# A fused attention and gated-MLP kernel: high and low parts for three output blocks of the first span, earlier key exponentials and later value loads for the third batch

## The chip, the cores and the metric

The kernel runs on one core of one Trainium2 chip. The metric is the device time of one execution in microseconds. A core has TensorE (PE, with its weight loads as PEld), VectorE (DVE), ScalarE (ACT), GpSimd (POOL) and SyncE (SP); SP and POOL issue the DMA transfers here.

## The reference

Linear attention over 8 batches and 8 heads (576 rows, 64 columns a head) feeds a gated MLP:

```python
q_s = exp(q - max(q, -1)) / (sum over the row + 1e-9)
k_s = exp(k - max(k, rows)) / (sum over the rows + 1e-9)
kv  = einsum('bhsd,bhse->bhde', k_s, v)
x   = einsum('bhsd,bhde->bhse', q_s, kv)       # then (4608, 512)
out = (sigmoid(x @ w_gate) * (x @ w_val)) @ w_out
```

The three weights are drawn as 64-bit floats (512 x 1536, 512 x 1536, 1536 x 512); everything else is float32, and so is the output of 4608 x 512.

## The kernel before, in words

The 4608 tokens are cut into nine spans of 512 (`w` = 0 to 8), the 1536 hidden columns into twelve blocks of 128 (`j`). Each engine works through its instructions in the order in which the program writes them; that order is written out by hand, and waits between engines follow from which tile is read and written where.

**The first span** (line 1024 on) runs the MLP block by block in full float32, because the weights only arrive and are narrowed from 64 to 32 bits while it runs. For one block: `g1_0` (line 672) computes gate and value sums of the block, eight products of 128x512; `g_sig_0` (680, ACT) takes the sigmoid of the gate, `g_mul_0` (684, DVE) multiplies it with the value sums into the tile `h_0`, one block later; `g2_0` (699) multiplies that by the block's rows of `w_out` and adds it into the four PSUM tiles `acc`. PE runs `g1_0` of block j and then `g2_0` of block j-1. The trace records a full float32 product as two instructions.

Beside that, block by block, the weights are made ready:
- `w_low`, `w_top`, `w_join` (146; 153 and 168; 175) narrow gate and value weights on DVE, ACT and DVE; `wo_low`, `wo_top`, `wo_join` do it for `w_out`.
- `wo_hi` (224, ACT) copies a `w_out` block to a high part, `wo_lo` (228, DVE) subtracts it for a low part, and `wo_store` (234, POOL) writes both to memory for the later spans. `wo_save` is the last two.
- after blocks 2, 5, 7, 9, 10 and 11, `split_hi` (284, ACT) and `split_lo` (289, DVE) split gate and value weights and their sums into high and low parts. The sums' parts sit in `s_sb`, and POOL stores them (294).

**The later spans** multiply such parts in three products (high x high, high x low, low x high) in a faster mode of PE: `g1` (line 717) does gate and value of two blocks at a time by seven sub-products B11, T1, T2, B21, T3, B22, T4 instead of eight, on weights `a_w` and sums `s_sb`; `g2` (785) does the output. A span takes six such stages. POOL reloads `s_sb` for the next stage (301) when a sub-product has read it, and `wo_hl`, `wo_t` (248) for the output.

**The attention of the next span** is woven between: for the second span, at the end of a block, `after_first` (889) puts in `k_mm` (424), the transposition `qf_tr` (549) and `x_mm` (587); at the next block's start `beside_first` (881) puts in `x_ev` (595, ACT copies x out of PSUM) and `qT_split` (562 on ACT, 563 on DVE: high and low part of the scaled q). `g1_0` and the transposition share three PSUM tiles `gv`, so a `g1_0` can start its second half only when the q of its block has been split. For the third batch `load_next` loads the transposed keys (320, SP), takes their maxima (330, DVE) and exponentials (337, ACT) two heads' pairs at a time, and at its step 5 loads q, k and the values v (481, 355, 368, all SP). The values are read by `k_mm` in the third stage of the second span.

SP takes its loads and stores in program order, too: an issue that waits holds all that stand behind it.

Of the kernel before, what the change touches and what calls it, by code (L numbers as in the profile page):

```python
# [8 lines left out]
F32 = mybir.dt.float32  # L9
F32R = mybir.dt.float32r  # L10
# [4 lines left out]
ALU = mybir.AluOpType  # L15
AX = mybir.AxisListType

P = 128
# [3 lines left out]
T = 512  # L22
# [4 lines left out]
NJ = DF // P  # L27
# [24 lines left out]
def attn_moe(ctx: ExitStack, tc: tile.TileContext, qf, qn, qT, k, kT, v, wg, wv, wo, out):  # L52
    nc = tc.nc
# [9 lines left out]
    two = ctx.enter_context(tc.tile_pool(name="two", bufs=2))  # L63
# [20 lines left out]
    v_two = [const.tile([P, DM], F32, name=f"v_{i}") for i in range(2)]  # L84
# [8 lines left out]
        out=kv_sb.rearrange("p b i h e -> p (b i) (h e)"),  # L93
        in_=kv_0.rearrange("p h e -> p (h e)").unsqueeze(1).broadcast_to([P, 4, DM]),
# [22 lines left out]
    wo_t = {}  # L117
# [32 lines left out]
    def narrow_sign(raw):  # L150

        half = raw.bitcast(F16).rearrange("p (e f) -> p e f", f=4)
        nc.scalar.activation(
            half[:, :, 1], words(raw)[:, :, 1].bitcast(F32), AF.Copy, scale=2.0 ** -100
        )
# [8 lines left out]
    def narrow_abs(raw, w):  # L164
        src = words(raw)[:, :, 1].bitcast(F32)
        if len(w.shape) == 3:
            src = src.rearrange("p (a b) -> p a b", a=w.shape[1])
        nc.scalar.activation(w, src, AF.Abs, scale=2.0 ** -112)
# [24 lines left out]
    def w_top(j):  # L193
        narrow_sign(w_raw[j].rearrange("p n e -> p (n e)"))
        for n in range(2):
            narrow_abs(w_raw[j][:, n], w_f32(j, n))

    def w_join(j, *ns):
        for n in ns or range(2):
            narrow_join(w_raw[j][:, n], w_f32(j, n))  # L200
# [9 lines left out]
    def wo_top(j):  # L210
        if j % 2 == 0:
            wo_t[j // 2] = wtpool.tile([P, 2, DM], F32, name="wo_t")
        if not wo_on_vector(j):
            narrow_sign(wo_raw[j])
        narrow_abs(wo_raw[j], wo_t[j // 2][:, j % 2])

    def wo_join(j):
        narrow_join(wo_raw.pop(j), wo_t[j // 2][:, j % 2])

    wo_out = {}  # L220
# [15 lines left out]
    def wo_save(j):  # L236
        wo_lo(j)
        wo_store(j)
# [119 lines left out]
    def v_load(b, t, vt=None):  # L358
        s0, n = KTILES[t]
        if vt is None:  # L360

            if t < 2:
                vt = v_two[t]
            else:
                vt = f_last[:, t - 2].rearrange("p n e -> p (n e)")
        v_sb[b, t] = vt
        src = v[b, s0:s0 + n]
        nc.sync.dma_start(out=vt[:n], in_=src)
# [190 lines left out]
    def qT_split(w, hp):  # L559
        t = qT_sb.pop((w, hp))  # L560
        hi, lo = (ring.tile([P, T], F32R, name="ring") for _ in range(2))
        nc.scalar.copy(out=hi, in_=t)
        nc.vector.tensor_tensor(out=lo, in0=t, in1=hi.bitcast(F32), op=ALU.subtract)
        qT_hl[w, hp] = (hi, lo)
# [95 lines left out]
    acc = {}  # L660


    h_0 = {}
    gate = {}

    def g1_0(j):
        ps = [ps_gv.tile([P, T], F32, name="gv") for _ in range(2)]
# [8 lines left out]
        gate[j] = ps  # L676

    def g_sig_0(j):
        h_0[j] = two.tile([P, T], F32, name="h_0", tag="h_lo")
        nc.scalar.activation(h_0[j], gate[j][0], AF.Sigmoid)  # L680

    def g_mul_0(j):
        g = h_0[j]
        nc.vector.tensor_tensor(out=g, in0=gate.pop(j)[1], in1=g, op=ALU.mult)

    def acc_new(w):
        acc[w] = [ps_acc.tile([P, DM], F32, name="acc") for _ in range(NT)]
# [7 lines left out]
    def g2_0(j):  # L695
        if j == 0:
            acc_new(0)
        for m in range(NT):
            nc.tensor.matmul(  # L699
                acc[0][m], lhsT=h_0[j][:, m * P:(m + 1) * P], rhs=wo_t[j // 2][:, j % 2],  # L700
                start=(j == 0), stop=(j == NJ - 1),
            )
        if j == NJ - 1:
            acc_out(0)

# [146 lines left out]
    def load_next(n, p, vs=range(5)):  # L852

        if n + 1 >= NW:
            return
        b = n + 1 if n + 1 < B else None
        if b is not None:
            if p == 1:
                kT_load(b, 0); kT_load(b, 1)
            if p == 2:  # L860
                k_max(b, 0); k_max(b, 1)
            if p == 3:
                k_sum(b, 0); k_sum(b, 1)
                kT_load(b, 2); kT_load(b, 3)
            if p == 4:
                k_max(b, 2); k_max(b, 3)
                k_max_send(b)
                if n > 1:
                    k_max_read(b)
        if p == 5:  # L870
            for c in range(NC):
                qn_load(n + 1, c)
            if b is not None:
                for t in range(5):
                    k_load(b, t)
                for t in vs:
                    v_load(b, t)

    def beside_first(j):
        if 7 <= j <= 10:
            x_ev(1, j - 7)
        if 6 <= j <= 9:
            qT_split(1, j - 6)
        if j == 6:
            k_done(1)

    def after_first(j):
        if j == 0:  # L890
            for hp in range(NP):
                k_max(1, hp)
            k_max_send(1)
        if j == 1:
            for t in range(5):
                v_load(1, t, v1[t])
            for c in range(NC):
                qn_max(1, c)
            k_max_read(1)
        if j == 2:  # L900
            for c in range(NC):
                qn_sub(1, c)
        if j == 3:
            for c in range(NC):
                qn_exp(1, c)
            for hp in range(NP):
                k_sum(1, hp)
            for t in range(5):
                k_sub(1, t)
        if j == 4:  # L910
            for t in range(5):
                k_exp(1, t)
            for c in range(NC):
                qn_sum(1, c)
        if 4 <= j <= 7:
            qf_mul(1, j - 4)
        if j == 5:
            for t in range(5):
                k_mm(1, t)
        if 6 <= j <= 9:  # L920
            x_mm(1, j - 6)
        if 5 <= j <= 8:
            qf_tr(1, j - 5, ps_gv.tile([P, T], F32, name="gv"))
        if j in (2, 6, 7, 9):
            load_next(1, {2: 1, 6: 2, 7: 3, 9: 4}[j])


    def lend(i):
# [95 lines left out]
    for j in range(NJ - 2):  # L1024
        g1_0(j)
        beside_first(j)
        split = splits.get(j)
        if split is not None:
            split_hi(split)
        if j == 0:  # L1030
            g_sig_0(j)
        else:
            wo_hi(j - 1)
            g_mul_0(j - 1)
        w_top(j + 2)
        if j > 0:
            g_sig_0(j)
        w_join(j + 1)
        wo_top(j + 1)
        wo_join(j)  # L1040
        if j + 3 < NJ:
            w_low(j + 3)
        wo_low(j + 2)
        if j > 0:
            wo_save(j - 1)
        if j + 3 < NJ:
            load_wo(j + 3)
        if j + 5 < NJ - 1:
            load_w(j + 5)
        if j == 7:  # L1050
            load_w(NJ - 1)
        if split is not None:
            split_lo(split)
        if j + 1 in splits:
            w_sums(splits[j + 1])
        if j > 0:
            g2_0(j - 1)
        if j == 3:
            kv_split(0, lambda sl: kv_0[sl, :, sl])
        after_first(j)  # L1060

    j = NJ - 2
# [22 lines left out]
    g_sig_0(j + 1)  # L1085
    split_hi(5, SUMS)
    c_subs()
    load_next(1, 5, range(2))
    c_split_lo(B11)
    split_lo(5, (FIRST,))  # L1090
    split_lo(5, SUMS[0:1])
# [13 lines left out]
    wo_hi(j + 1)  # L1105
    wo_lo(j + 1)
    g2_0(j)
    for t in range(2, 5):
        v_load(2, t)

    def wo_next(w, at):
        wo_load(w, step(w, at))
# [2 lines left out]
    for w in range(1, NW):  # L1115
        last = w == NW - 1
        for at in range(NS):
            p = step(w, at)
            end = last and at == NS - 1
            g1(w, p, None if end else step(w + (at + 1) // NS, (at + 1) % NS))  # L1120
            if prev is None:
                wo_store(NJ - 1)
            ahead = 3 if at == NS - 1 and not last else 0
            for i in range(ahead):
                c_split(i)
            h_split(w, p)
            if ahead:
                for i in range(ahead, 7):
                    c_split(i)
            if not last:  # L1130
                side_a(w + 1, at)
            if prev is None:
                g2_0(NJ - 1)
                wo_hl[1, NS - 1] = [wo_out[j] for j in (NJ - 2, NJ - 1)]
            else:
                g2(*prev)
                if prev == (1, 0):
                    wo_next(1, 1)
                if not end:
                    wo_next(w + (at + 1) // NS, (at + 1) % NS)  # L1140
            prev = (w, at)
            if not last:
                side_b(w + 1, at)
# [39 lines left out]
```

## Time and profile before

| | |
|---|---|
| median of 3 runs | 928.67 us (928.15 to 929.54) |
| the profiled execution's own time | 928.82 us |
| its span, first to last instruction | 927.1 us |
| granted clock of PE | 0.998 |
| PE busy | 919.4 us (99%) |
| DVE, ACT, POOL busy | 619.1, 488.7, 177.2 us |
| moved by DMA | 256.77 MB, 277 GB/s in the mean |

All times in the views count from the first instruction. The first span ends on PE at about 166 us, with the products of line 699 for its last block at 169.5. A busy PE is not PE at its peak: matmuls overlap, and their ends are modelled; the chain of waits gives the time from one group's start to the next.

### The profile page before, as it was taken

The page shows a single profiled execution, that of the slowest core. Times are in us where ns is not written, and L with a number is a line of the kernel's source. Part 1 is how long each engine was busy: PE and PEld are TensorE (multiplying, and loading weights), DVE is VectorE, ACT ScalarE, POOL GpSimd, SP SyncE. Part 2 cuts the span into 40 slices and gives each one's busy share as a digit, 9 for nine tenths or more (in the row PEclk, how much of TensorE's full clock was granted, in tenths as well). Part 3 has the DMA queues.
Part 4 walks back from the last instruction along what each step waited for, and adds up shares of the span by engine and source line. Part 5 has one row for each costly group of instructions (what it writes and reads, how often), then busy time and mean ns, then how long its engine had stood idle before and what let it go on. Part 6 is the DMA issues. An engine that isn't in the chain of part 4 may idle for free.

```text
span 927.1 us, 16312 instructions
## 1 busy us (share of the span) xinstructions
PE 919.4 (99%) x6366; PEld 793.9 (86%) x6366; DVE 619.1 (67%) x1005; ACT 488.7 (53%) x830; POOL 177.2 (19%) x329
## 2 busy tenths in 40 slices
PE   8999999999999999999999999999999999999998
PEld 7445445899999999999999999999999999899997
DVE  7899889865768476757775677656855574654232
ACT  5999885735454544644564456444634443543222
POOL 0011113222121212121221222112211222122220
PEclk9999999999999999999999999999999999999999
DMA  9996676999799969996999699969997799768661
GB/s 331 380 376 255 238 269 238 360 340 283 205 373 323 273 192 372 334 281 183 360 342 282 200 333 333 300 203 310 334 298 219 222 260 317 227 190 257 209 206 68
DMA packets 92507, 256.77 MB, mean 277 GB/s; under 512 B 13648, under 2 KB 13648, under 8 KB 92432
## 3 DMA queue, kind: packets, MB, share of 16 engines
q0 software_dynamic: 46016, 167.27, 57.8%
q1 hardware_dynamic: 46416, 88.48, 31.5%
q8 instruction: 50, 0.82, 0.4%
q14 instruction: 25, 0.20, 0.1%
HBM read 227.15 MB, written 28.56 MB: 276 GB/s over the span
## 4 chain that ended last, share of the span: by engine, by line
PE 98%; DMA 1%; SPq 0%; ACT 0%; issue 0%
PE gv L717 49%; PE acc L785 29%; PE gv L672 9%; PE acc L699 4%; PE at L424 2%; PE gv L587 2%; PE at L587 1%; DMA lent<-v_in 1%; DMA lent<-qf_in 1%; PE gv L549 0%; PE acc L611 0%; PE acc L410 0%; PE at L410 0%; SPq L948 0%; SPq L951 0%; ACT x L691 0%
## 5 line engine op out<-in xcount | busy, mean ns | idle before, releaser
L717 PE MATMUL gv<-c_hl,s_sb 128*128 128x256 f32 x2304 | 277.5, 276 | 0.0
L717 PEld LDWEIGHTS gv<-c_hl,s_sb 128*128 128x128 f32 x2304 | 269.0, 188 | 0.0
L717 PE MATMUL gv<-c_hl,a_w 128*128 128x256 f32 x1728 | 220.9, 277 | 0.0
L717 PEld LDWEIGHTS gv<-c_hl,a_w 128*128 128x128 f32 x1728 | 210.4, 188 | 4.6 <-issue 0.7
L301 POOL DMA_DIRECT2D s_sb<-s x188 | 101.7, 541 | 305.6 <-PE gv L717 297.9
L785 PE MATMUL acc<-wo_hl,h 128*128 128x512 f32 x588 | 142.6, 391 | 0.0
L743 DVE TENSOR_TENSOR sg<-gv,sg 128x512 f32<-128x512 f32 x48 | 33.2, 691 | 158.8 <-PE gv L717 158.8
L785 PE MATMUL acc<-wo_t,h 128*128 128x512 f32 x564 | 138.9, 394 | 0.0
L785 PEld LDWEIGHTS acc<-wo_t,h 128*128 128x128 f32 x564 | 105.8, 188 | 24.8
L785 PEld LDWEIGHTS acc<-wo_hl,h 128*128 128x128 f32 x588 | 106.9, 188 | 20.5
L735 ACT COPY sg<-gv 128x512 f32<-128x512 f32 x48 | 28.1, 586 | 111.0 <-PE gv L717 97.7
L745 ACT COPY sg<-gv 128x512 f32<-128x512 f32 x48 | 28.2, 588 | 102.7 <-PE gv L717 102.7
L747 DVE TENSOR_TENSOR sg<-sg 128x512 f32<-128x512 f32 x48 | 33.3, 693 | 57.3 <-ACT sg L745 57.3
L672 PE MATMUL gv<-x,f_w 128*128 128x512 f32 x160 | 70.4, 593 | 0.0
L248 POOL DMA_DIRECT2D wo_hl<-wo x47 | 27.7, 590 | 182.6 <-PE acc L785 182.6
L672 PEld LDWEIGHTS gv<-x,f_w 128*128 128x128 f32 x160 | 30.0, 190 | 36.6 <-issue 34.4
L768 DVE TENSOR_TENSOR h<-sg,h 128x1024 fp32r<-128x1024 f32 x48 | 58.9, 1226 | 1.6
L756 DVE TENSOR_TENSOR sg<-sg 128x512 f32<-128x512 f32 x48 | 33.3, 693 | 33.6 <-ACT sg L750 33.6
L750 ACT ACTIVATE sg<-sg 128x512 f32<-128x512 f32 x48 | 30.4, 633 | 46.1 <-DVE sg L749 46.1
L740 ACT COPY sg<-gv 128x512 f32<-128x512 f32 x48 | 28.2, 588 | 37.3 <-PE gv L717 37.3
L737 ACT COPY sg<-gv 128x512 f32<-128x512 f32 x48 | 28.2, 588 | 36.3 <-PE gv L717 36.3
L248 POOL DMA_DIRECT2D wo_t<-wo x47 | 25.4, 540 | 99.1 <-PE acc L785 99.0
(148 smaller groups left out, 1120.8 us busy)
## 6 DMA issues: line engine op xcount, KB each, us to landing
s_sb<-s POOLq DMA_DIRECT2D x188, 512.0 KB, 6.4
wo_hl<-wo POOLq DMA_DIRECT2D x47, 512.0 KB, 4.3
wo_t<-wo POOLq DMA_DIRECT2D x47, 512.0 KB, 6.1
s<-s_sb POOLq DMA_DIRECT2D x24, 512.0 KB, 6.9
out<-x SPq DMA_DIRECT2D x36, 256.0 KB, 6.9
ring<-k_in SPq DMA_DIRECT2D x28, 256.0 KB, 8.8
ring<-qn_in SPq DMA_DIRECT2D x28, 256.0 KB, 5.9
q_b<-q_m_row SPq DMA_DIRECT2D x56, 128.0 KB, 9.6
```

Source lines behind the costliest of these rows:

```text
L248: nc.gpsimd.dma_start(out=t.rearrange("p h e -> p (h e)"), in_=wo_dram[2 * p + i].bitcast(F32R))
L301: nc.gpsimd.dma_start(out=s_sb[:, i].rearrange("p h n e -> p (h n e)"), in_=s_dram[p][:, i * n:(i + 1) * n].bitcast(F32R),)
L672: nc.tensor.matmul(ps[n], lhsT=w[:, kt // 2, sl], rhs=x_0[:, kt], start=(kt == 0), stop=(kt == NK - 1),)
L699: nc.tensor.matmul(acc[0][m], lhsT=h_0[j][:, m * P:(m + 1) * P], rhs=wo_t[j // 2][:, j % 2], start=(j == 0), stop=(j == NJ - 1),)
L717: nc.tensor.matmul(ps[:, n], lhsT=lh(kt), rhs=c_hl[i][:, x, kt], start=(first and n == 0 and kt == 0 and lh is wh and x == 0), stop=(last ...
L737: nc.scalar.copy(out=sg[:, 2], in_=z)
L743: nc.vector.tensor_tensor(out=sg[:, 0], in0=rr, in1=sg[:, 0], op=ALU.add)
L747: nc.vector.tensor_tensor(out=sg[:, 3], in0=sg[:, 3], in1=sg[:, 2], op=ALU.add)
L750: nc.scalar.activation(sg[:, 0:2, 0], sg[:, 0:2, 0], AF.Sigmoid)
L756: tt(out=sg[:, 0:2, 0], in0=sg[:, 0:2, 0], in1=sg[:, 0:2, 1], op=ALU.mult)
L768: nc.vector.tensor_tensor(out=lo, in0=sg[:, :, 0], in1=hi.bitcast(F32), op=ALU.subtract)
L785: nc.tensor.matmul(acc[w][m], lhsT=h[lh][:, i, sl], rhs=o[i][:, rh], start=(at == 0 and i == 0 and lh == 0 and rh == 0), stop=(at == NS - ...
```

## The change

It has three parts.

1. For blocks 6, 7 and 8, `g2_0` uses high and low parts. The sigmoid and its product go to one of the two tiles `v_two` (which hold two of the second batch's value tiles earlier, and two of the third batch's later); a new ACT copy `h_hi_0` and a new DVE subtraction `h_lo_0` split that into `h_parts`; the parts of `w_out` that `wo_hi` and `wo_lo` make anyway are the other factor. So that `wo_lo` is there in time, `wo_save` moves up to before `wo_top`, and `h_lo_0` stands behind it. Four products per block become twelve.
2. `beside_first` puts `qT_split` ahead of `x_ev`. The third batch's steps move: the first exponentials and the second maxima one block earlier each (step 3 from the end of block 7 to that of block 6, step 4 from 9 to 8), and the first maxima (step 2) from the end of block 6 into its middle.
3. Loading the third batch's values moves from the end of the first span (two tiles with step 5, three behind block 10's output products) to behind the output products of block 11, in the next stage.

```diff
+    def in_parts(j):
+        return 6 <= j <= 8
...
     def g_sig_0(j):
-        h_0[j] = two.tile([P, T], F32, name="h_0", tag="h_lo")
+        h_0[j] = v_two[j % 2] if in_parts(j) else two.tile([P, T], F32, name="h_0", tag="h_lo")
...
+    def h_hi_0(j):
+        h_parts[j] = t = two.tile([P, 2, T], F32R, name="h_parts", tag="h_lo")
+        nc.scalar.copy(out=t[:, 0], in_=h_0[j])
+
+    def h_lo_0(j):
+        hi, lo = (h_parts[j][:, i] for i in range(2))
+        nc.vector.tensor_tensor(out=lo, in0=h_0[j], in1=hi.bitcast(F32), op=ALU.subtract)
...
     def g2_0(j):
...
+        if in_parts(j):
+            (h_hi, h_lo), (o_hi, o_lo) = ([t[:, i] for i in range(2)] for t in (h_parts[j], wo_out[j]))
+            pairs = [(h_hi, o_hi), (h_hi, o_lo), (h_lo, o_hi)]
+        else:
+            pairs = [(h_0[j], wo_t[j // 2][:, j % 2])]
         for m in range(NT):
-            nc.tensor.matmul(
-                acc[0][m], lhsT=h_0[j][:, m * P:(m + 1) * P], rhs=wo_t[j // 2][:, j % 2],
-                start=(j == 0), stop=(j == NJ - 1),
-            )
+            for i, (h, o) in enumerate(pairs):
+                nc.tensor.matmul(
+                    acc[0][m], lhsT=h[:, m * P:(m + 1) * P], rhs=o,
+                    start=(j == 0), stop=(j == NJ - 1 and i == len(pairs) - 1),
+                )
...
     def beside_first(j):
+        if 6 <= j <= 9:
+            qT_split(1, j - 6)
         if 7 <= j <= 10:
             x_ev(1, j - 7)
-        if 6 <= j <= 9:
-            qT_split(1, j - 6)
...
-        if j in (2, 6, 7, 9):
-            load_next(1, {2: 1, 6: 2, 7: 3, 9: 4}[j])
+        if j in (2, 6, 8):
+            load_next(1, {2: 1, 6: 3, 8: 4}[j])
...
             g_mul_0(j - 1)
+            if in_parts(j - 1):
+                h_hi_0(j - 1)
         w_top(j + 2)
...
         w_join(j + 1)
+        if in_parts(j - 1):
+            wo_save(j - 1)
+            h_lo_0(j - 1)
         wo_top(j + 1)
+        if j == 6:
+            load_next(1, 2)
         wo_join(j)
...
-        if j > 0:
+        if j > 0 and not in_parts(j - 1):
             wo_save(j - 1)
...
-    load_next(1, 5, range(2))
+    load_next(1, 5, ())
...
-    for t in range(2, 5):
-        v_load(2, t)
...
                 g2_0(NJ - 1)
+                for t in range(5):
+                    v_load(2, t)
```

On ACT, from the end of block 6 into block 7, before: the x copy and the q copy (595, 562), the six split copies, `wo_hi` of block 6, the weights of block 9, the sigmoid of block 7 (a tile `h`), and then the table load and the exponentials.

```order
L168 ACTIVATE wo_t<-wo_raw 128x512
L595 COPY x_114<-at 128x512
L562 CAST ring<-gv 128x512
...
L284 CAST a_w<-f_w 128x512
L224 CAST wo_hl<-wo_t 128x512
L153 ACTIVATE w_raw<-w_raw 128x1024
L168 ACTIVATE f_w<-w_raw 128x2x256 x2
L680 ACTIVATE h_864<-gv 128x512
L153 ACTIVATE wo_raw<-wo_raw 128x512
L168 ACTIVATE wo_t<-wo_raw 128x512
L337 ACT_TABLE_LOAD
```

The same place now (lines of the changed kernel: 684 is the sigmoid, 692 is `h_hi_0`):

```order
L168 ACTIVATE wo_t<-wo_raw 128x512
L337 ACT_TABLE_LOAD
L337 ACTIVATE kt_119,k_sum<-kt_119,k_neg 128x576
L337 ACTIVATE kt_120,k_sum<-kt_120,k_neg 128x576
L562 CAST ring<-gv 128x512
L595 COPY x_114<-at 128x512
...
L224 CAST wo_hl<-wo_t 128x512
L692 CAST h_parts<-v_117 128x512
L153 ACTIVATE w_raw<-w_raw 128x1024
L168 ACTIVATE f_w<-w_raw 128x2x256 x2
L684 ACT_TABLE_LOAD
L684 ACTIVATE v_118<-gv 128x512
```

The exponentials moved ahead of block 7's copies, the table load back to the sigmoid's set moved ahead of block 7's sigmoid (before, it stood ahead of block 8's), and the copy of `h_parts` stands behind `wo_hi`.

On DVE in block 7, before: the q subtraction, the product of block 6, the joins, the low bits of the next weights, and then `wo_lo` (228) ahead of the split.

```order
L563 TENSOR_TENSOR ring<-gv,ring 128x512
L684 TENSOR_TENSOR h_792<-gv,h_792 128x512
L175 SCALAR_TENSOR_TENSOR f_w<-f_w,w_raw 128x2x256 x2
L175 SCALAR_TENSOR_TENSOR wo_t<-wo_t,wo_raw 128x512
L146 TENSOR_SCALAR sg<-sg 128x1024
L146 TENSOR_SCALAR wo_raw<-wo_raw 128x512
L159 SCALAR_TENSOR_TENSOR wo_raw<-wo_raw 128x512
L228 TENSOR_TENSOR wo_hl<-wo_t,wo_hl 128x512
```

And now (688 is the product, 696 is `h_lo_0`):

```order
L563 TENSOR_TENSOR ring<-gv,ring 128x512
L688 TENSOR_TENSOR v_117<-gv,v_117 128x512
L175 SCALAR_TENSOR_TENSOR f_w<-f_w,w_raw 128x2x256 x2
L228 TENSOR_TENSOR wo_hl<-wo_t,wo_hl 128x512
L696 TENSOR_TENSOR h_parts<-v_117,h_parts 128x512
L175 SCALAR_TENSOR_TENSOR wo_t<-wo_t,wo_raw 128x512
L146 TENSOR_SCALAR sg<-sg 128x1024
L146 TENSOR_SCALAR wo_raw<-wo_raw 128x512
L159 SCALAR_TENSOR_TENSOR wo_raw<-wo_raw 128x512
```

`wo_lo` has overtaken four instructions, and `h_lo_0` is new behind it.

On SP at the end of the first span, before: keys, values, the row of q maxima, the output's stores, the spreading of the q maxima.

```order
L355 DMA ring<-k_in 64x512
L368 DMA v_117<-v_in 128x512
L368 DMA v_118<-v_in 128x512
L368 DMA f_last<-v_in 128x512 x2
L368 DMA f_last<-v_in 64x512
L487 DMA q_m_row<-q_m 128x32
L692 DMA out<-x_114 128x512 x4
L527 DMA q_b<-q_m_row 64x512 x8
```

And now (704 is the output's store):

```order
L355 DMA ring<-k_in 64x512
L487 DMA q_m_row<-q_m 128x32
L704 DMA out<-x_114 128x512 x4
L368 DMA v_117<-v_in 128x512
L368 DMA v_118<-v_in 128x512
L368 DMA f_last<-v_in 128x512 x2
L368 DMA f_last<-v_in 64x512
L527 DMA q_b<-q_m_row 64x512 x8
```

The five value loads moved behind the row of maxima and the four stores of the first span's output.

More of the change, by code (lines that the diff above doesn't have):

```diff
@@ L663, in attn_moe @@
     h_0 = {}
+    h_parts = {}
     gate = {}
+    def in_parts(j):
+        return 6 <= j <= 8
     def g1_0(j):
```

## The prediction

> **What bounds the kernel now.** I read the page first, then the waits of TensorE (PE), then the chain of waits in order of time, then the timelines of ScalarE (ACT), VectorE (DVE) and the DMA issues around blocks 6 to 9 of the first span. From the page, the busy shares and the chain by engine:
>
> ```profile
> PE 919.4 (99%) x6366; PEld 793.9 (86%) x6366; DVE 619.1 (67%) x1005; ACT 488.7 (53%) x830; POOL 177.2 (19%) x329
> ...
> PE 98%; DMA 1%; SPq 0%; ACT 0%; issue 0%
> ```
>
> All waits of PE (engine, line, what it waited for, us in total, times, longest):
>
> ```profile
> PE acc L394 <- ACT lent L337: 2.2, 2, 1.9
> PE gv L975 <- POOL lent L943: 1.1, 1, 1.1
> PE at L410 <- DMA lent<-v_in: 0.3, 1, 0.3
> ```
>
> These three lie in the prologue. From block 0 to the end PE never stands idle, so the kernel costs what PE's instructions cost, and a microsecond less of them is a microsecond of time as long as everything else arrives that much earlier too. The chain in order of time (start us, us, what):
>
> ```profile
> 101.05 6.87 PE gv L672 x16
> 107.92 3.43 PE acc L699 x8
> 111.36 0.95 PE at L587 x6
> 112.30 0.44 PE gv L549 x4
> 112.74 7.08 PE gv L672 x16
> 119.81 3.43 PE acc L699 x8
> ...
> 156.48 9.54 PE gv L717 x84
> ...
> 194.47 2.63 PE at L424 x80
> ...
> 212.40 5.53 PE acc L785 x24
> ```
>
> One block of the first span is g1_0 (6.87), g2_0 (3.43) and, in blocks 6 to 9, x_mm (0.95) and a transposition (0.44). The g1_0 of block 8 took 7.08, 0.21 over the others.
>
> **The change, part by part.**
>
> *PE.* In g2_0 of blocks 6, 7 and 8 four full-precision products (eight recorded halves, 3.43 us) become twelve on high and low parts. Their like is line 785: the same 128x512 shape, the same reading of high and low parts, two blocks in 24 instructions of 5.53 us, so 5.53 / 24 = 0.230 each and 12 x 0.230 = 2.77 a block. The saving is 3 x (3.43 - 2.77) = 1.98 us, all on the path. That such products keep their pace among full-precision ones is borne out by x_mm, which already runs them there: its six hold 3 x 512 columns in 0.95. Bounds: 0.230 exact, 1.98; paced like x_mm's columns (0.95 / 3 = 0.317 for 512), 12 x 0.317 = 3.80 and a loss of 1.1 over three blocks. I take the first: same shape, and x_mm's is a 64-column piece beside each 448.
>
> The Trainium skill, "FP8 and Floating Point Precision", TensorE Precision Notes, gives a full FP32 product four passes through the array; three would be three quarters, 2.57 a block and an estimated 2.57 us for all three. The trace differs (2.77 to 3.43 is 0.81), and the row decides.
>
> *ACT and DVE.* Each of the three blocks adds an ACT copy (h_hi), like wo_hi in line 224, and a DVE subtraction (h_lo), like wo_lo in line 228. g2_0 now waits for both and for wo_lo, which it did not need before. ACT around block 7 (start us, us):
>
> ```profile
> 97.12 0.70 ACT L168 ACTIVATE wo_t<-wo_raw 128x512 f32<-128x512 f32 x1
> 100.70 0.59 ACT L595 COPY x<-at 128x512 f32<-128x512 f32 x1 [2.88 <-issue]
> 101.66 2.19 ACT L284 CAST s_sb<-s 128x512 fp32r<-128x512 f32 x4
> 103.74 1.57 ACT L284 CAST a_w<-f_w 128x1024 fp32r<-128x1024 f32 x2
> 105.21 0.62 ACT L224 CAST wo_hl<-wo_t 128x512 fp32r<-128x512 f32 x1
> 105.73 2.51 ACT L153 ACTIVATE w_raw<-w_raw 128x1024 f16<-128x1024 f32 x1
> 107.98 1.28 ACT L168 ACTIVATE f_w<-w_raw 128x512 f32<-128x512 f32 x2
> 109.17 0.58 ACT L680 ACTIVATE h<-gv 128x512 f32<-128x512 f32 x1
> 111.46 1.28 ACT L337 ACT_TABLE_LOAD   x1
> 112.75 0.78 ACT L337 ACTIVATE kt<-kt,k_neg 128x576 f32<-128x576 f32 x1
> 114.28 0.56 ACT L595 COPY x<-at 128x512 f32<-128x512 f32 x1
> ```
>
> The table load and the two exponentials (111.46 to 114.28, 2.82) move one block forward, into the 2.88 us in which ACT stood idle before 100.70: from 97.8 to 100.6. Then the q copy goes ahead of the x copy; it waits for the transposition, which ends at 101.05 by the chain, so the six split copies start at about 102.06, 0.4 later than now. They take 3.55 (101.66 to 105.21): wo_hi runs from 105.6 to 106.23, h_hi (0.52 behind it) ends at 106.75. DVE at the same place:
>
> ```profile
> 103.09 1.30 DVE L175 SCALAR_TENSOR_TENSOR f_w<-f_w,w_raw 128x512 int32<-128x512 int32 x2
> 104.29 0.70 DVE L175 SCALAR_TENSOR_TENSOR wo_t<-wo_t,wo_raw 128x512 int32<-128x512 int32 x1
> 106.59 0.69 DVE L228 TENSOR_TENSOR wo_hl<-wo_t,wo_hl 128x512 fp32r<-128x512 f32 x1
> ...
> 111.34 0.68 DVE L543 TENSOR_TENSOR ring<-ring,q_r 128x512 f32<-128x512 f32 x1
> 115.37 0.69 DVE L563 TENSOR_TENSOR ring<-gv,ring 128x512 fp32r<-128x512 f32 x1 [3.34 <-ACT ring L562]
> ...
> 125.33 0.69 DVE L563 TENSOR_TENSOR ring<-gv,ring 128x512 fp32r<-128x512 f32 x1 [2.80 <-ACT ring L562]
> ```
>
> DVE is through with the joins at 104.29 and now meets wo_lo: it waits two microseconds for wo_hi, until about 106.3, with everything behind it queued (wo_join, w_low, wo_low, split_lo, the q product). h_lo ends near 107.6. PE asks for the block's first product at 107.92, for h_lo two products later at 108.4: no wait, 0.8 to spare. In block 8 no split copies stand in front, and it is easier. In block 9 they do: with PE's new times the transposition ends at 123.1, two copies and the 3.55 put wo_hi's end at 128.3 and h_lo's at 129.6, and PE asks for h_lo at 130.4, again 0.8 to spare.
>
> Two more waits of PE touch this. g1_0 of block 8 starts at 107.92 + 2.77 + 0.95 + 0.44 = 112.08 and needs the sigmoid of block 7, which now has h_hi and the table load in front: 106.65 + 2.25 + 1.19 + 1.29 = 111.38, with its 0.58 ended at 111.96, 0.1 to spare. Its second half needs the q subtraction of line 563. That is what the 0.21 were (115.37 + 0.69 = 116.06 for a half asked for at 112.74 + 3.43 = 116.17, the handover included). Now DVE comes to it without the 3.34 of waiting: from 107.5, the work between wo_lo's successor at 107.19 (106.59 + 0.60) and the end of line 543's slot at 111.94 is 4.75; the ops that wo_lo has overtaken, by the rows from 104.29 to 106.59, are 2.30; so line 563 runs from 107.5 + 2.30 + 4.75 = 114.55 to 115.24, for a half asked for at 115.51. I count the 0.21 as gone.
>
> Where DVE's time comes from: the idle 3.34 and 2.80 go, 6.14 in all, against 3 x 0.60 for h_lo and twice 2.0 of waiting for wo_hi, 5.8. So DVE reaches the tail of the span where it does now, and PE comes 2.2 earlier. There DVE hands over the parts of the next span, one of them and its use:
>
> ```profile
> 155.96 0.69 DVE L651 TENSOR_TENSOR c_hl<-ring,c_hl 128x512 fp32r<-128x512 f32 x1
> ...
> 157.69 2.88 PE L717 MATMUL gv<-c_hl,s_sb 128*128 128x256 f32 x24
> ```
>
> This is T2's low part, ready at 156.65; T2 is the second dozen of the 24, at 157.69 + 1.36 = 159.05. Of 2.4 to spare 0.2 to 0.5 are left: enough, barely.
>
> The moved k_max, kT loads and the kmax row cost nothing: the reductions' readers, the exponentials, stand behind the block's weight work, and PE reads none of it before the next span; uncovered, they would hold DVE no longer than they do now. On SP the two kT loads wait for exponentials that end at 100.6, and the wo load queued behind them waits for a join after 104.29 anyway; on POOL the kmax row overtakes one wo store whose data comes later still.
>
> *The values.* s_sb is reloaded at the end of the span; the S1 load, then its use, then the DMA share in this stretch, then the longest landing near by:
>
> ```profile
> L301 POOL DMA_DIRECT2D s_sb<-s x1: 545/545/545, 160.7 to 160.7; - x1
> ...
> DMA to landing us min/median/max: 9.8/9.8/9.8
> ...
> 170.70 2.99 PE L717 MATMUL gv<-c_hl,s_sb 128*128 128x256 f32 x24
> ...
> 156.00:170.00 14.00, 14.00 (x101) 11.85 (x100) 11.97 (x21) 7.38 (x15) 3.76 (x8) 1.00 1.03 371
> ...
> 172.26 2.37 SPq L692 DMA_DIRECT2D out<-x  x4
> ...
> L320 SPq DMA_DIRECT2D kt<-kT_in x2: 328/375/422, 190.9 to 192.2; - x2
> ...
> DMA to landing us min/median/max: 13.3/13.3/13.4
> ```
>
> It lands at 170.5 and is used at 170.7: 0.2 to spare, with the DMA engines full (share 1.03, 371 GB/s). With PE 2.2 earlier it would cost 2.0. But the five value loads (4.5 x 256 KB = 1.18 MB, 3.2 us at 371 GB/s), issued among the stores that S1 queues behind, are gone from here: it lands near 167.3 for a use at 168.5. Bounds: no sooner, a wait of 2.0; 3.2 sooner, none. I take none, since a full pipe with less in it is done sooner. The values now stand behind the four output stores (174.6 less 2.2), land by the longest row within 13.3 us of an issue at 172.4 to 175, so by 188.5, and their readers, the k products of line 424, start at 194.47 less 2.2 = 192.3. They put 3.2 us of transfers ahead of the next s_sb loads, which have a stage, 9.54 + 5.53 less a product, from issue to use, and land within about 10.
>
> **Sum.** 1.98 + 0.21 = 2.2 off the profiled execution, which took 928.82 (span 927.1 and 1.7 around it). The median of the runs is 928.67, 0.15 lower; I predict 928.67 - 2.2 = 926.5.
>
> **The rivals.**
> *Thin cover.* wo_lo and h_lo in blocks 7 and 9, block 7's sigmoid, T2: four places with 0.1 to 0.8 to spare, each a microsecond of PE for a microsecond of lateness. If ACT or DVE is 0.5 to 1 later than I walked it, half to 1.4 of the gain goes: 927.0 to 927.9. For it: the spares; against: every duration is from its own row. Chance 0.17.
> *S1 lands no sooner.* The stores it follows wait for DVE, which is no earlier. PE waits 2.0: 928.5. Chance 0.08.
> *The table switch.* If ACT needed more after the load than its row, the sigmoid of block 7 would hold g1_0: 1.4 late is 1.3 of waiting, 927.8. The row says 111.46 + 1.28 = 112.74 and the next exponential at 112.75. Chance 0.02. The Trainium skill, "ScalarE: Activation LUTs", What ACT_TABLE_LOAD costs, adds a drain of about 1.38 us to each switch; this row does not show it.
> *Slower: the values come too late.* They stand in one queue behind the output stores and share a full pipe with s_sb and wo. The k products read them at 192.3. Each microsecond after that is one lost, and from 4.1 on (196.4, a landing 21 us after issue) the kernel is slower by over 0.2%: landing at 198.8 gives 933.0. No landing around takes over 13.4. Chance 0.04.
> *It does less than it says.* Parts paced like x_mm's: 928.67 + 1.1 - 0.2 = 929.6. Chance 0.03.
> The forecast keeps 0.66.
>
> **Numbers.** 0.2% of 928.67 is 1.86, about what a measurement of this kernel can tell from no change: faster ends at 926.81, only 0.3 above the forecast. The runs before spread over 1.4, so their medians move by some 0.4. Of the forecast's 0.66 I give 0.54 to faster, of thin cover 0.03: 0.57. Slower 0.04, the rest, 0.39, within. The range: 926.5 less 0.4 for the medians and 0.3 for pace, 925.8; up through thin cover, 928.1.
>
> **What would show it.** Right: g2_0 of blocks 6 to 8 at 2.77 in the chain, g1_0 of block 8 at 6.87, PE still without waits after the prologue, the stage after the span beginning 2.2 earlier, DVE's 3.34 and 2.80 gone and two waits on line 224 in their place. Wrong: a PE wait on h_parts, wo_hl or s_sb; g2_0 above 3; k products that wait for the values.

## The result, and the profile after

| | before | after |
|---|---|---|
| median, 9 runs each | 928.15 us (927.55 to 932.32) | 935.14 us (931.12 to 941.12) |
| ratio, 95% interval | | 1.0080 (1.0056 to 1.0104) |
| profiled execution, its span | 928.82, 927.1 us | 934.73, 932.8 us |
| granted clock of PE | 0.998 | 0.994 |

The kernel became 0.8% slower, 7 us above the 928.15 before and beyond the upper end of the forecast (926.5, 925.8 to 928.1). All waits of PE after (engine, line, what it waited for, us in total, times, longest):

```profile
PE gv L735 <- ACT sg L753: 4.9, 1, 4.9
PE gv L993 <- POOL lent L961: 1.1, 1, 1.1
PE acc L394 <- ACT lent L337: 1.0, 1, 1.0
PE at L410 <- DMA lent<-v_in: 1.0, 3, 0.7
```

The last three lie in the prologue as before. The first is new, and it does not lie where the products were changed. The chain of after in order of time (start us, us, what) tells where it is:

```profile
110.47 1.28 ACT L684
...
111.77 0.61 ACT v L684
...
112.42 7.13 PE gv L676 x16
119.55 2.73 PE acc L717 x12
...
130.53 2.77 PE acc L717 x12
...
154.85 9.54 PE gv L735 x84
...
192.99 2.63 PE at L424 x80
...
216.44 1.52 PE gv L735 x12
...
223.71 0.48 ACT sg L753
...
224.23 8.97 PE gv L735 x60
233.20 5.53 PE acc L803 x24
```

Up to the k products (192.99, before 194.47) PE is ahead of the kernel before. It then stands idle for 4.92 us up to 224.23 (from 219.31), and the 60 products behind the wait take 8.97 where an undisturbed stage's 84 take 9.52, so 60 x 9.52 / 84 = 6.80. The product of line 803 at 233.20 stood at 227.45 before: 5.75 later, and the spans differ by 932.8 - 927.1 = 5.7. All of the loss is in this one place. The granted clock there (the figure ahead of the last two in each row; the first are the window, its length and the busy times):

```profile
217.00:224.00 7.00, 2.31 (x21) 2.11 (x19) 5.62 (x9) 6.49 (x13) 1.27 (x2) 0.82 1.14 282
224.00:228.00 4.00, 3.77 (x17) 3.77 (x18) 0.69 (x1) 1.25 (x3) 0.54 (x1) 0.50 0.51 168
228.00:232.00 4.00, 4.00 (x36) 4.00 (x35) 1.50 (x3) 1.46 (x2) 0.54 (x1) 0.97 0.47 131
```

The clock was granted at half for the four microseconds after the idling.

Why ACT's copy (line 753) came late is read backwards. DVE after (start us, us, and in brackets the idle time before it and what ended it):

```profile
211.91 0.76 DVE L330 TENSOR_REDUCE k_max<-kt 128x1 f32<-128x576 f32 x1 [3.01 <-DMA kt<-kT_in]
214.69 0.76 DVE L330 TENSOR_REDUCE k_max<-kt 128x1 f32<-128x576 f32 x1 [1.84 <-DMA kt<-kT_in]
215.56 0.69 DVE L761 TENSOR_TENSOR sg<-gv,sg 128x512 f32<-128x512 f32 x1
```

and the same work before:

```profile
205.49 0.76 DVE L330 TENSOR_REDUCE k_max<-kt 128x1 f32<-128x576 f32 x1 [0.24 <-DMA kt<-kT_in]
...
208.43 0.69 DVE L743 TENSOR_TENSOR sg<-gv,sg 128x512 f32<-128x512 f32 x1 [2.00 <-PE gv L717]
```

DVE takes the maxima of the fourth batch's keys ahead of the sums that empty PE's PSUM tile. Before, it was through with them at 206.4 and waited 2.00 us for PE; after, the second pair of keys lands at 214.67 instead of 205.46, and line 761 waits for the maxima. Behind line 761 come DVE's other sums, ACT's sigmoids, a table load and six exponentials, and only then the copy that PE needs. The keys are late because of SP. Its loads after (start of the first, us from first to last, how many):

```profile
172.91 2.23 SPq L368 DMA_DIRECT2D v<-v_in  x2
175.24 1.62 SPq L368 DMA_DIRECT2D f_last<-v_in  x3
178.05 13.15 SPq L527 DMA_DIRECT2D q_b<-q_m_row  x8
...
193.41 4.62 SPq L534 DMA_DIRECT2D ring<-qT_in  x4
198.34 1.60 SPq L320 DMA_DIRECT2D kt<-kT_in  x2
```

and before, where the five values were long done:

```profile
176.12 7.13 SPq L527 DMA_DIRECT2D q_b<-q_m_row  x8
...
189.02 1.86 SPq L534 DMA_DIRECT2D ring<-qT_in  x4
190.93 1.61 SPq L320 DMA_DIRECT2D kt<-kT_in  x2
```

The eight spreads of the q maxima stand right behind the values and now take 13.15 us to be issued instead of 7.13; the transposed q and the keys behind them start 4.4 and 7.4 us later. From the first spread to the second pair of keys, each issue of SP comes 0.02 to 0.09 behind the landing of the transfer eight places before it: spreads at 182.23, 184.47 and 187.08 behind values that landed at 182.21, 184.45 and 187.06. So SP has eight transfers under way here, and the ninth waits. The trace's records of the issues name the reason: the program gives SP's transfers eight semaphores in turn (101, 103 to 106, 108 to 110), and each issue waits for the semaphore that the transfer eight places before it raises. The eight is thus a limit of the program; whether more semaphores would help was not tried.

### The profile page after: what moved, and what is told of

The parts are those of the page before. It is cut to its first block, busy times and chain, and to the rows that moved or that the text cites. A ratio compares the mean times of both kernels' runs of the same rounds, so it can differ in the third digit from the quotient of the medians.

```text
span 932.8 us, 16340 instructions
## 1 busy us (share of the span) xinstructions
PE 920.5 (99%) x6378; PEld 798.5 (86%) x6378; DVE 620.3 (66%) x1008; ACT 489.6 (52%) x833; POOL 177.3 (19%) x329
## 4 chain that ended last, share of the span: by engine, by line
PE 96%; ACT 2%; DMA 1%; SPq 0%; issue 0%; ACTq 0%
PE gv L735 49%; PE acc L803 29%; PE gv L676 8%; PE acc L717 4%; PE at L424 2%; PE gv L587 2%; PE at L587 1%; DMA lent<-v_in 1%; DMA lent<-qf_in 1%; PE acc L410 0%; PE acc L611 0%; PE gv L549 0%; PE at L410 0%; ACT w_raw L153 0%; ACT ring L553 0%; SPq L966 0%
## 6 DMA issues: line engine op xcount, KB each, us to landing
q_b<-q_m_row SPq DMA_DIRECT2D x56, 128.0 KB, 9.4
```

## The experiments

The prologue differs between executions: block 4's `g1_0` starts at

```profile
65.39 7.03 PE L672 MATMUL gv<-x,f_w 128*128 128x512 f32 x16
```

before, and after at

```profile
65.58 7.03 PE L676 MATMUL gv<-x,f_w 128*128 128x512 f32 x16
```

and elsewhere between 63.96 and 65.93. So the profiled executions are compared from that row on. "Last landing" is the later of the keys and the transposed q, less that start; "wait" is PE's near 218; "60 products" is the time of those behind it (6.80 where none waited, as above); "end" is the span less that start.

| kernel | median us | ratio to before (95%) | last landing | wait | 60 products | end |
|---|---|---|---|---|---|---|
| before | 928.15 | | 140.07 | none | 6.80 | 861.7 |
| after | 935.14 | 1.0080 (1.0056 to 1.0104) | 149.09 | 4.9 | 8.97 | 867.2 |
| e1 values back | 927.63 | 0.9994 (0.9985 to 1.0003) | 143.66 | none | 6.80 | 861.4 |
| e2 values alone | 934.76 | 1.0074 (1.0053 to 1.0095) | 151.08 | 4.9 | 9.88 | 870.2 |
| e3 values by GpSimd | 927.09 | 0.9995 (0.9984 to 1.0005) | 145.37 | 1.1 | 7.08 | 861.5 |
| e4 keys by GpSimd | 931.51 | 1.0038 (1.0026 to 1.0050) | 145.83 | 2.5 | 8.71 | 864.8 |
| e5 an eighth of the values | 927.15 | 0.9978 (0.9967 to 0.9990) | 145.16 | 1.0 | 7.08 | 861.4 |
| e6 fill a stage ahead | 931.00 | 1.0034 (1.0021 to 1.0048) | 148.31 | none | 7.33 | 864.9 |
| e7 values and keys by GpSimd | 926.35 | 0.9978 (0.9966 to 0.9990) | 140.12 | none | 6.80 | 859.9 |
| e8 high and low parts alone | 929.78 | 1.0017 (1.0002 to 1.0031) | 141.89 | none | 6.80 | 863.5 |
| e9 values ahead of the stores | 928.82 | 1.0007 (0.9991 to 1.0023) | 144.66 | 0.7 | 7.33 | 861.2 |
| e10 fill in the wait | 932.21 | 1.0038 (1.0023 to 1.0052) | 151.04 | 0.8 | 7.08 | 867.3 |

The kernel before took 927.96 to 928.37 in the medians beside these runs, and the ratios of e1 to e10 are to those.

Single executions differ. The last landing is 140.07 to 143.66 in the three whose values are loaded early (before, e1, e8) and 148.31 to 151.08 in the four that load them late on SP behind the stores (after, e2, e6, e10). The spreads take 7.13 to 8.09 us to be issued in those three and 13.15 to 15.42 in these four, and counted from block 4 the first keys are issued at 125.5 to 128.0 and at 132.8 to 135.1. Only what lies outside such a range is read as an effect.

**e1, the values back in their old place** (parts 1 and 2 of the change alone):

```diff
-    load_next(1, 5, ())
+    load_next(1, 5, range(2))
...
+    for t in range(2, 5):
+        v_load(2, t)
...
-                for t in range(5):
-                    v_load(2, t)
```

> The changed kernel with the third batch's values loaded where the kernel before loads them; the other two parts stay. Queue theory (the five value loads, standing ahead of the q spreads among SyncE's loads, make the q rows, the transposed q and the transposed keys land up to 9 us later, and PE idles 4.9 us for it and then runs at half its clock): no wait of PE over 1 us after the prologue, clock about 0.998, 926.5 to 927. Early-PE theory (the loss comes from PE being 1.6 us earlier against transfers that cannot be): the wait near 218 us stays, 930 or more. If the s_sb loads at the span's end land no sooner without the move, PE waits up to 2 us for them near 168 us: 928.5.

The wait near 218 is gone, and another stands in front:

```profile
159.22 9.81 DMA s_sb<-s
...
169.16 8.42 PE gv L735 x72
```

PE waited 1.4 us for the S1 reload, which landed at 169.03; counted from block 4 that is 104.95, where after's landed at 101.30 (166.88). That is the wait for which the values were moved away: parts 1 and 2 gain 1.8 and give 1.4 of it back.

**e2, the values alone** (part 3 of the change, put into the kernel before; the inverse of the diff above).

> The kernel before with the late value loads alone. Queue theory: the second transposed key tile lands near 214 us as in the changed kernel instead of 205.5, but PE asks 1.6 us later, so it idles about 3 us near 220 us, and the clock adds 1 to 2: 931 to 933. Early-PE theory: the spare time is still there, no wait, 928.

The chain of its profile goes through the whole line of causes:

```profile
176.34 13.92 DMA f_last<-v_in
...
190.28 10.09 DMA q_b<-q_m_row
...
200.38 15.14 DMA kt<-kT_in
...
215.55 0.76 DVE k_max L330
...
225.09 9.88 PE gv L717 x60
```

With PE at its old pace the loss is as large as with all three parts, and larger than expected: the wait is 4.9 instead of 3. That the transfers are late only because PE is early is refuted; part 3 by itself is the loss.

**e3, the late values issued by GpSimd:**

```diff
-                    v_load(2, t)
+                    v_load(2, t, eng=nc.gpsimd)
```

> The changed kernel with the five late value loads issued by GpSimd at the same place of the program, behind the sums' reload, instead of by SyncE. Queue theory: SyncE's loads go out as before, the values land near 175 us, no wait of PE: 926.5 to 927. Bytes theory (1.18 MB moved behind the span's end delay whatever follows, whoever issues them): the q rows and keys still land several us late, PE still idles 2 us or more: 929 to 932.

Nearly all of it is back. GpSimd issued the values at 166.72 to 168.88, 6.2 to 7.5 us sooner than SP had, and they landed by 176.81; a wait of 1.1 stays. The bytes theory was right in one thing. With the values off SP, the spreads still took longer than the 7.13 to 8.09 of early values:

```profile
176.43 10.00 SPq L527 DMA_DIRECT2D q_b<-q_m_row  x8
```

The keys landed 5.3 later than in the kernel before, by the table, and the waits further on took up most of that: PE's is 1.1.

**e4, the first keys of the fourth batch by GpSimd:**

```diff
-            nc.sync.dma_start(out=t, in_=kT[b, hp * P:(hp + 1) * P])
+            eng = nc.gpsimd if b == 3 and hp < 2 else nc.sync
+            eng.dma_start(out=t, in_=kT[b, hp * P:(hp + 1) * P])
```

> The changed kernel with the fourth batch's first two transposed key tiles loaded by GpSimd instead of SyncE; the values stay late. If these keys are the last link (VectorE's maxima wait for them and hold the stage's PSUM additions, and those hold ScalarE and PE): the additions start on time, no wait of PE over 1 us: 926.5 to 928. If the transposed q and the spread rows are the link: the wait near 218 us stays at 3 us or more: 931 or more.

About half, between the two expectations. With the keys there at 199.5, the transposed q stands last, through another reader on DVE (the chain):

```profile
197.35 13.25 DMA ring<-qT_in
...
210.63 0.69 DVE ring L539
...
221.63 8.71 PE gv L736 x60
```

So the keys are not the only link: the transposed q, which SP also held behind the values, is one too.

**e5, an eighth of the values' bytes:**

```diff
-        src = v[b, s0:s0 + n]
-        nc.sync.dma_start(out=vt[:n], in_=src)
+        cols = D if b == 2 else DM
+        src = v[b, s0:s0 + n, :cols]
+        nc.sync.dma_start(out=vt[:n, :cols], in_=src)
```

> The changed kernel, but its five late value loads take only the first 64 of 512 columns, an eighth of the bytes, from the same places in SP's queue. It leaves out seven eighths of the third batch's values. Theory A (places in the queue: every issue of SP waits for the landing of the one eight before it, however small that is): the q spreads and the keys still come late, the last kT lands at 211 us or later, TensorE waits 3 us or more for sg, 931 us or more. Theory B (the bytes: the 16 DMA engines carry the values first): the values land within 2 to 3 us, the last kT by 208 us, the wait is under 1.5 us, 928.5 us or less.

The time speaks for the bytes. The spreads (lines are one later here):

```profile
175.91 10.12 SPq L528 DMA_DIRECT2D q_b<-q_m_row  x8
```

10.12 lies midway between 7.13 and 13.15, and the small values still took 7.7 to 10.5 us to land, not the 2 to 3 expected. Counted from block 4, the first keys are issued at 127.2, as with early values (125.5 to 128.0). The last landing, 145.16, lies 3.2 to 5.9 ahead of the executions with late values on SP behind the stores and 1.5 to 5.1 behind those with early ones. By the time and by the keys' issue the bytes are nearly all of it; what the five places cost by themselves is not clear of the spread.

**e9, the values on SP, but ahead of the four stores:**

```diff
+                for t in range(5):
+                    v_load(2, t)
                 g2_0(NJ - 1)
-                for t in range(5):
-                    v_load(2, t)
```

> The changed kernel with the five late value loads still on SP, but in its queue ahead of the four out stores instead of behind them. Theory M (the moment: the values cost because their 1.2 MB are asked for after 172.9 us, just ahead of the q spreads): issued some us sooner they behave as the ones that GpSimd issued at 166.7 to 168.9 us, the last kT lands by 211 us, TensorE waits 1 to 2 us near 218 us, 926.5 to 928.5 us. Theory Q (SP's queue: its issues wait for the landing of the one eight before, whatever the moment): the stores and the q spreads are pushed back as far as in the changed kernel, the wait stays over 3.5 us, 932 us or more.

The queue and the bytes are those of after, with only the order of values and stores exchanged (the chain, then the spreads):

```profile
175.38 11.42 DMA out<-x
...
186.81 11.44 DMA q_b<-q_m_row
...
198.27 12.32 DMA kt<-kT_in
...
220.17 7.33 PE gv L735 x60
```

```profile
178.04 11.22 SPq L527 DMA_DIRECT2D q_b<-q_m_row  x8
```

The values are issued 1.8 to 3.2 us sooner (171.09 to 173.21, after 172.91 to 176.37), and 6.3 of the 7 us are back in the median. The expectation for the moment said up to 928.5; it came to 928.82, over a wide spread (926.28 to 934.53). So SP as such is not the wrong queue; the values' place in it counts. How the place works is shown in part only. Four stores, 1.0 MB, now stand right ahead of the spreads, which still take 11.22, and the first keys are issued at 131.05 from block 4, sooner than the 132.8 of after but later than with early values. The keys then took 11.2 and 12.3 us to land, for 13.5 and 15.1 in the changed kernel, and why is not known. The Trainium skill, "DMA: Bandwidth & Descriptors", Issuing engines are not separate DMA queues, says that transfers share the same 16 engines whoever issues them, and that another issuer saves only the time of issuing, usually little. The trace of e3 agrees with the sharing: the spreads took 10.00 although GpSimd had the values. The saving was not little here: e3 brought 8.0 us, as what stood behind the values on SP went out sooner, and an earlier place on SP (e9) brought 6.3.

**e6 and e10, work for the idle PE.** Eighteen products of the identity with itself, read by nobody, first a stage too early (e6), then in the wait itself (e10):

```diff
+        if (w, p) == (1, 3):
+            fill = ps_at.tile([P, T], F32, name="at")
+            for _ in range(18):
+                nc.tensor.matmul(fill[:, 0:P], lhsT=ident, rhs=ident, start=True, stop=True)
         prod(y, wsum(S2), T2, False, False)
```

with `(1, 2)` in e6.

> The changed kernel with 18 products of the identity with itself put on TensorE ahead of the product that waits at 218 us; nobody reads them. Theory of the clock (the 60 products after the wait took 8.97 us where 60 x 0.1134 = 6.8 because the granted clock fell to 0.50 after 4.9 us of idling): with TensorE busy through most of the wait the clock stays at 0.95 or more between 217 and 236 us, the 2.2 us go and the time is 932.5 to 933.5 us. If the low clock comes from something else, it stays at 935 us and the 60 products at 8.5 us or more.

> The changed kernel with the 18 products of the identity in the stage that waits, between the last product ahead of the wait and the one that waits for sg (in the run before they came one stage sooner, and TensorE met its data 4 us later). The fill took 4.05 us there and the wait is 4.9. Theory of the clock (idling costs the 2.2 us behind the wait): the wait is under 1.5 us, the 60 products take 6.8 to 7.3 us instead of 8.97, and the time is 932.5 to 933.5 us. If the slow products have another cause, they stay at 8.5 us or more and it is 935 us.

My place in e6 was wrong: the fill ran at 202.55, one stage ahead of the wait, so it pushed PE back by its 4 us, and PE met its data almost on time. Even so the kernel became 4.1 us faster in the median (931.00 against 935.14; 2.3 in the ends of the profiled executions) for doing 4 us more. In e10 the fill stands where PE waits (start us, us, idle before in brackets):

```profile
220.31 4.18 PE L760 MATMUL at<-ident 128*128 128x128 f32 x36
225.30 1.64 PE L735 MATMUL gv<-c_hl,s_sb 128*128 128x256 f32 x12 [0.82 <-ACT sg L753]
```

```profile
225.30 7.08 PE gv L735 x60
```

The clock stayed at 1.00, and the 60 products took 7.08 instead of 8.97. So the clock is 1.9 of the 2.17 behind the wait. The other 0.3 also stands behind the short waits of e3 and e5, and 0.5 in e6 and e9, all at full clock. The profiled execution of e10 ends where after's does: its keys happened to land 1.95 later, and PE waited another 1.54 just ahead of the fill. The medians differ by 2.9.

**e8, the high and low parts alone** (as e1, and the exponentials, maxima and x copies in their old order too):

```diff
+        if 7 <= j <= 10:
+            x_ev(1, j - 7)
         if 6 <= j <= 9:
             qT_split(1, j - 6)
-        if 7 <= j <= 10:
-            x_ev(1, j - 7)
...
-        if j in (2, 6, 8):
-            load_next(1, {2: 1, 6: 3, 8: 4}[j])
+        if j in (2, 6, 7, 9):
+            load_next(1, {2: 1, 6: 2, 7: 3, 9: 4}[j])
```

> The high and low parts alone: the exponentials, the x loads and the values stand as before the change. Theory that part 2 pays (the exponentials were moved to take the wait of block 8's g1_0 away): waits of 0.5 to 1 us on TensorE at blocks 7 and 8, and the S1 reload's wait of about 1.4 us, 927.0 to 928.0 us. Rival, that part 2 is worth nothing: no such waits, the same 927.6 us as with the values alone put back.

The waits are there, at block 8 and at the S1 reload, none at block 7:

```profile
PE gv L735 <- DMA s_sb<-s: 1.5, 1, 1.5
PE gv L676 <- DVE ring L563: 1.1, 1, 1.1
```

The time is 929.78, worse than expected: part 1 without part 2 is no faster than before. Against e1 (861.4 from block 4) this end is 2.1 later; 1.0 of that is there behind block 8, 1.7 behind the S1 reload, and all of it at the k products.

**e7, values and first keys both by GpSimd** (the edits of e3 and e4 together):

> The changed kernel with the late values and the first two kT loads of batch 3 both issued by GpSimd. If the queue of SP is the whole loss, no wait of TensorE over 0.5 us is left behind the prologue, and what is left is the gain of the first span: 928.0 less 1.6 to 2.2, that is 925.8 to 926.4 us. If GpSimd's transfers merely take the same DMA engines from the q spreads at another moment, a wait of 1 us stays near 218 us and it is 927 us.

No wait of PE behind the first span, in the stage that waited as in the one before it:

```profile
200.14 9.52 PE gv L736 x84
...
215.19 9.52 PE gv L736 x84
```

926.35 us, 0.22% faster than before (0.10% to 0.34%), and the fastest kernel of the study with the whole computation. Its end, 859.9 from block 4, is 1.8 less than before's 861.7: the gain of the first span, and nothing else.

## Why the prediction was wrong

*The products of blocks 6 to 8* held: 2.73 and 2.77 in the chain, as line 785 had priced them. Neither the x_mm price of 3.80 nor the estimate of 2.57 was seen.

*The 0.21 of block 8* did not go, though its reason did: line 563 ran at 114.72 without a wait (I had 114.55). Its `g1_0` took 7.13, and it started on block 7's sigmoid, which ended at 111.77 + 0.61 = 112.38 where I had 111.96 (46.80 and 46.57, counted from block 4). The waits of e4, e5 and e7 list 0.2 to 0.3 us of PE on this sigmoid. The first span's gain is (156.48 - 65.39) - (154.85 - 65.58) = 1.82 instead of 2.2. This is one of the four places of the rival of the thin cover, and the 0.4 lost is just short of the 0.5 at which I had it begin.

*The other covers* held. PE waits for neither `wo_hl` nor `h_parts` nor T2's low part. DVE's 3.34 and 2.80 went, and two waits on line 224, 1.95 and 2.04, stand in their place, as predicted. e8 adds what I had not priced: without part 2, 2.1 of the gain would have been lost. Which of its moves does that was not tried. And *the table switch* was as its row said: load 1.28, the sigmoid 0.01 behind it.

*The S1 reload* was right: 166.88 (I had 167.3), no wait. That it would have waited without part 3 is shown by e1 (1.4; I had 2.0).

*The values for the k products* were right too: landed by 190.75 (I had 188.5), read from 192.99, no wait. The slower rival asked the right question of the wrong reader.

*The step that failed* is the last of the part on the values: "They put 3.2 us of transfers ahead of the next s_sb loads, which have a stage". It had both the readers and the size wrong. I followed the values to their own readers and to GpSimd's s_sb loads, and to nothing that stands behind them on SP. The order in the section on the change shows the eight q spreads directly behind, and behind those come the transposed q and the keys of the fourth batch, with readers on DVE that stand ahead of PSUM's emptying. Three rows of before would have given most of their spare: DVE's 2.00 us ahead of line 743, quoted above, DVE's next wait, for a copy of ACT, and ACT's wait for PE ahead of the copy that PE needs:

```profile
210.34 0.69 DVE L747 TENSOR_TENSOR sg<-sg 128x512 f32<-128x512 f32 x1 [1.22 <-ACT sg L745]
...
219.32 0.59 ACT L735 COPY sg<-gv 128x512 f32<-128x512 f32 x1 [1.27 <-PE gv L717]
```

After, the keys landed 9.2 later. DVE's 2.00 took up some of it (line 761 ran at 215.56 for 208.43, 7.13 later), the two other waits took up 2.8 more (the copy ran at 223.62 for 219.32, 4.30 later), and PE asked for it sooner. These rows alone would have shown the way, but not the sign. The three waits come to 4.5; with PE 2.2 earlier that leaves 2.3, so 3.2 us of transfers would have cost 0.9 at most, less than the gain. The size was wrong too: counted from block 4, the first keys were issued at 132.76 for 125.54, 7.2 later, and not 3.2, because SP's issues wait, by the program's semaphores, for landings eight places back, and these came later as well.

e2 shows this step alone to be worth the whole loss, e4 that keys and transposed q are both links, and e3, e5, e7 and e9 that all or most of it goes when the values are sooner, smaller or out of the way.

*A size I did not foresee at all* is the clock: 1.9 us on top of a wait of 4.9.

What stays open: why a transfer's time from issue to landing varies as it does (the keys that SP issued took 13.3 us before, 13.5 to 15.1 after, and 11.2 to 16.4 over the other runs). The bytes and the queue of eight account for the direction, not for each transfer's time, and e10's keys landed 1.95 later than after's with the same loads ahead of them. This spread from execution to execution is a likely reason that after's runs reach from 931 to 941 us; that was not tried.

## What to carry to other kernels

A load that is moved can be paid for by what stands behind it in its new queue: list the next sixteen issues of that queue, find each one's reader, and see what stands behind that reader on its own engine up to the next thing that the bounding engine needs; the spare is about the sum of the waits on that way, less what the bounding engine gains. Do not price the delay by the bytes alone: 3.2 us of transfers became 7.2 us at the issue of the keys. Here the move cured a wait of 1.4 us and set off one of 4.9. Where PE is the bound, count an idle stretch of a few microseconds with a surcharge for the clock, 1.6 to 2.8 us here over what short waits cost.

## What the runs showed of the hardware that was not expected

The clock. Wait of PE and time of the next 60 products: none 6.80 (7.33 in e6), 0.7 us 7.33, 0.8 to 1.1 us 7.08, 2.5 us 8.71, 4.9 us 8.97 and 9.88. Up to 1.1 us the clock stayed at 1.00. In e4, behind a wait of 2.5 us:

```profile
222.00:224.00 2.00, 2.00 (x11) 2.00 (x11) 0.69 (x1) 0.05 (x1) 0.00 (x0) 0.50 1.10 399
```

The Trainium skill, "TensorE: Matmul & The Clock Gate", HAM oscillation, gives the rule of no idle gaps over about 3.4 us. The 4.9 us agree with it; the 2.5 us of e4 are below it and brought the half clock too, so here gaps of 1.4 and 1.5 (e1, e8 and e10, clock 1.00) left the clock alone and one of 2.5 did not.

Small transfers in a full pipe are not quick: an eighth of the values' bytes landed after 7.7 to 10.5 us, where the whole values took 9.3 to 14.4 in the changed kernel.
